# Two attention layers and two GLU layers on one core: four value parts folded instead of three, and the second output projection in two strips

## The chip, the core and the metric

The kernel runs on one core of a Trainium2 chip. The metric is the device time of one execution in microseconds, median over runs; lower is better. The core has TensorE (PE), VectorE (DVE), ScalarE (ACT), GpSimd (POOL) and SyncE (SP), which here only issues transfers. 16 DMA engines bring data from HBM into SBUF.

## The reference

Everything is float32. Two tokens (B = 2, one position each) pass through attention, a GLU block, the same attention again and the same GLU block again, each with a layer norm before it and a residual around it:

```python
def _A_ref(x, k_cache, v_cache, wq, wo):
    B, Sq, D = x.shape                      # 2, 1, 576
    H, Dh = 32, 128                         # caches: (2, 32, 8192, 128)
    q = (lambda x, *d: x.transpose(*d))((x @ wq).reshape(B, Sq, H, Dh), 0, 2, 1, 3)
    scores = jnp.einsum("bhqd,bhkd->bhqk", q, k_cache) * (Dh ** -0.5)
    p = _softmax(scores, axis=-1)
    o = jnp.einsum("bhqk,bhkd->bhqd", p, v_cache)
    return (lambda x, *d: x.transpose(*d))(o, 0, 2, 1, 3).reshape(B, Sq, H * Dh) @ wo

x = x + _A_ref(_layernorm(x, axis=-1), A_k_cache, A_v_cache, A_wq, A_wo)
x = x + _B_ref(_layernorm(x, axis=-1), B_w_gate, B_w_up, B_w_down)
x = x + _A_ref(_layernorm(x, axis=-1), A_k_cache, A_v_cache, A_wq, A_wo)
x = x + _B_ref(_layernorm(x, axis=-1), B_w_gate, B_w_up, B_w_down)
```

`_B_ref` is gelu(x @ w_gate) * (x @ w_up) @ w_down with an inner width of 4608. Each attention layer reads K and V of all 64 pairs of batch and head, 512 MB.

## The kernel before

**Items.** An attention layer goes through items in a fixed order, the second layer in the reverse order of the first. An item is two heads of one batch (30 items that `PAIRS` counts, the kernel's numbers 0 to 29) or one head (4 items, the end of layer 0 and the start of layer 1). K and V of a two-head item are 8 MB each; they lie in SBUF as 128 partitions of 128 rows of 128 numbers, cut into eight parts of 16 rows (`JC`; a part is 2048 numbers a partition).

**Scores.** `multiply` (L769) lets VectorE multiply K by the query, which is held in PSUM, in place, in three steps of three, three and two parts (6144, 6144 and 4096 numbers a partition). GpSimd then adds the upper half of each row to the lower (L798), and VectorE sums what is left to one score a row (`add_up`, L801). `peak` (L825), `highest` (L833) and `softmax` (L850 to L858) turn scores into weights in the tile `prz`, with small matmuls (L827, L835, L871) in between.

**Values.** PE multiplies the weights by V (`values`, L943), four matmuls of 512 columns a part, each into its own strip of 32 partitions of the accumulator `acc`. The last `FOLD` parts of V are not multiplied by PE in the items that `folds` names (numbers 3 to 26 in layer 0, 2 to 26 in layer 1, 49 in all). For those, `weigh` lets VectorE multiply V by the weights, which ScalarE has copied to PSUM as `share` (L905, multiplication at L911), and GpSimd adds the rows together in halves (L914) down to four rows; `folded` then adds these four rows with one matmul (L921). With `FOLD = 3` the first call of `weigh` takes one part, and the second two, and L916 joins the two.

**Order.** The engines run their instructions in the order in which the program writes them. In item n the loop writes: the last `add_up` and `peak` of the item before (p), the second `weigh` of the item before that (f), the first `multiply`, the next item's query (L687), `folded(f)`, the softmax of p, the second `multiply`, for every other item `gather` (L966, L967), for the others `inverse` (L877), `values` of p, the first `add_up`, the third `multiply`, the first `weigh` of p, the second `add_up`.

**Transfers.** SyncE issues all large transfers on one queue, in the order that `plan_first`, `plan_second` and `plan_mlp` write down, each as soon as its space is free. Space for the two-head items is three pairs of slots, each pair for one K or V. K of the next item (L168) goes where V of two items ago lay, so it waits for `folded`; V of this item goes where its own K lay, so it waits for its last `add_up`. An issue that waits holds up all issues behind it.

**Projection.** After the items, `project` multiplies the attention output (4 columns) by wo. In layer 1, wo comes in two pieces (`WIDE` is 16: 16 rows of 128, 576 columns), and each of the 16 rows is multiplied in four strips of 144 columns, one to each 32 partitions of `xps` (L1021). `add_to_x` (L589) adds the result to `x` in the same layout. Then the GLU of layer 1 begins: `norm`, and the gate and up products (L1203), whose weights are transferred in space that K, V and wo have left.

Of the kernel before, what the change touches and what calls it, by code (L numbers as in the profile page):

```python
# [15 lines left out]
P = 128  # L16
B = 2
# [3 lines left out]
D = 576  # L21
# [3 lines left out]
JC = 16  # L25
HALF = P // 2
# [9 lines left out]
CW = D // 4  # L36
# [7 lines left out]
END = RING + NPLACE * PLACE  # L44
HELD = 5
SPLIT = (18, 18, 12, 16)
FOLD = 3


class Item:  # L50
# [75 lines left out]
def decode_layers(ctx, tc, x_in, kc, vc, wq, wo, wg, wu, wd, out):  # L126
    nc = tc.nc
# [10 lines left out]
    x = consts.tile([P, CW], F32, name="x")  # L138
    nc.vector.memset(x, 0.0)
    for c in range(4):  # L140
        for s in range(2):
            lo = 32 * c + s * B
# [12 lines left out]
    def done(key):  # L155
        arena.free(key)
        pump()

    def part_at(at, n):
        return space[:, at:at + n]  # L160
# [177 lines left out]
    def groups(layer):  # L338
        return range(H // WIDE[layer])[::1 - 2 * layer]

    def name(kind, layer, n):

        return kind, 1 if n in (KEYS_HELD if kind == "k" else VALUES_HELD) else layer, n
# [119 lines left out]
    for b in range(B):  # L463
        rows = ident.rearrange("p (c v i r) -> p i r v c", c=4, v=4, i=2)[:, :, :, b, :]
# [38 lines left out]
    acc = psum1.tile([P, 2, 512], F32, name="acc")  # L503
# [5 lines left out]
    xps = bank[:, 0:CW]  # L509
# [6 lines left out]
    low = bank2[:, 4 * GH + P + 6:]  # L516
    share = low[:, :FOLD * JC]
    kept = psum1.tile([P, JC, DH], F32, name="kept")
# [69 lines left out]
    def add_to_x():  # L588
        nc.vector.tensor_add(x, xps, x)  # L589
# [22 lines left out]
    def attention(layer):  # L612
# [28 lines left out]
        if layer == 0:  # L641
            for us in GU[0]:
                w = ready.pop(("wq", 0, us[0])).rearrange("p (u w) -> p u w", w=4 * EQ)
# [193 lines left out]
        def weights_of(n):  # L837

            if ITEMS[n].heads == 2:
                return prz.rearrange("p a e -> p (a e)")  # L840
            return prz[:, n - PAIRS, :]
# [55 lines left out]
        def weigh(n, first):  # L897

            lo = ITEMS[n].parts - FOLD
            if first:  # L900
                of_halves = weights_of(n)[:, 8 + 4 * JC * lo:8 + 4 * JC * (lo + FOLD)]
                of_halves = of_halves.rearrange("p (g a e) -> p a g e", a=4, e=4)
                for i in range(2):
                    at = slice(i * HALF, i * HALF + HALF)
                    nc.scalar.copy(share[at].rearrange("p (g e) -> p g e", e=4), of_halves[at, i])  # L905
            begin, rows = (0, JC) if first else (JC, (FOLD - 1) * JC)
            at = arena.live[name("v", layer, n), lo][0]
            t = part_at(at, FOLD * PART).rearrange("p (j d) -> p j d", d=DH)
            of_rows = share[:, begin:begin + rows].unsqueeze(2).to_broadcast([P, rows, DH])
            u = t[:, begin:begin + rows]  # L910
            nc.vector.tensor_tensor(out=u, in0=u, in1=of_rows, op=ALU.mult)  # L911
            while rows > 4:
                rows //= 2
                nc.gpsimd.tensor_tensor(out=u[:, :rows], in0=u[:, :rows], in1=u[:, rows:2 * rows], op=ALU.add)  # L914
            if not first:
                nc.gpsimd.tensor_tensor(out=t[:, :4], in0=t[:, :4], in1=u[:, :4], op=ALU.add)  # L916

        def folded(n):

            key, lo = name("v", layer, n), ITEMS[n].parts - FOLD  # L920
            nc.tensor.matmul(  # L921
# [92 lines left out]
        def project(g):  # L1014

            w = ready.pop(("wo", layer, g)).rearrange("p (i c) -> p i c", c=D)
            n = WIDE[layer]
            o = oT.rearrange("p g i s b -> p (g i) (s b)")
            for i in range(n):
                for c in range(4):  # L1020
                    nc.tensor.matmul(  # L1021
                        xps[32 * c:32 * c + 2 * B, :], o[:, g * n + i, :], w[:, i, c * CW:(c + 1) * CW],
                        start=(g == groups(layer)[0] and i == 0), stop=(g == groups(layer)[-1] and i == n - 1),
                    )
            done(("wo", layer, g))
# [25 lines left out]
        for i, n in enumerate(seq):  # L1051
# [8 lines left out]
            first = layer == 1 and i == 1  # L1060
# [8 lines left out]
            if f is not None:  # L1069
                weigh(f, False)  # L1070
# [3 lines left out]
            for j, (k, m) in enumerate(us):  # L1074
# [28 lines left out]
                if j == 2 and i and folds(p):  # L1103
                    weigh(p, True)
# [12 lines left out]
        n, p = seq[-1], seq[-2]  # L1117
        add_up(n, *units(n)[-1])
        first, second = groups(layer)[:2]
# [5 lines left out]
        if layer == 0:  # L1125
            nc.scalar.copy(two, qs)
            project(first)
# [4 lines left out]
        if layer == 0:  # L1132
            project(second)

            third, fourth, fifth = groups(layer)[2:5]
            values(N - 1, 0, 2)
            for g in (third, fourth):
                project(g)
            for k in range(2, ITEMS[n].parts, 2):
                values(N - 1, k, k + 2)  # L1140
                if k + 2 == ITEMS[n].parts:
                    nc.scalar.copy(back, spare)
            gather(n)
            project(fifth)
            context(n)
            divide(n)
        else:
            values(N - 1)
            finish(n)
            regroup()  # L1150
        spread()
        for g in groups(layer)[5:] if layer == 0 else groups(layer):
            project(g)
        add_to_x()


    def write(engine):
# [3 lines left out]
    def mlp(layer):  # L1161
# [106 lines left out]
        if layer == 0:  # L1268
            idle_products(1, 0)

    attention(0)
    mlp(0)
    attention(1)
    mlp(1)
    write(nc.scalar)
# [27 lines left out]
```

## Time and profile before

| | |
|---|---|
| median of 3 runs | 2680.91 us (2680.71 to 2681.0) |
| profiled execution | 2680.4 us, span 2678.6 us |
| VectorE busy | 2086.9 us (78%) |
| GpSimd busy | 1797.4 us (67%) |
| PE busy | 848.9 us (32%) |
| read from HBM | 1152.39 MB |

The span is what the profiler saw from the first to the last instruction of the profiled execution. Busy shares are means over the whole span, in which attention fills all but the first part, a stretch in the middle and the last 100 us or so. The rows that the prediction quotes from the timeline give the start in us, the duration (of all instructions of a merged row), engine, line and operation, the tiles written and read with their shapes, and in brackets the idle time before it with what ended that.

### The profile page before, as it was taken

The numbers are of one execution on the slowest core, as the hardware profiler recorded it, in microseconds if no ns is written. First come the engines' busy times: TensorE is split into PE (matmuls) and PEld (weight loads), VectorE is DVE, ScalarE is ACT, GpSimd is POOL, SyncE is SP. The second block draws the span as 40 slices with busy tenths as digits, with TensorE's granted clock in tenths as the row PEclk, the third lists the DMA queues.
The fourth block names the chain that finished last, engine by engine and source line by source line (L and its number), as shares of the span: only waits on it lengthen the run. The fifth ranks groups of instructions, "written<-read, shape, count | busy, mean of one in ns | idle before, by whom it ended". The sixth has DMA issues, their size and how long they took to land.

```text
span 2678.6 us, 14389 instructions
## 1 busy us (share of the span) xinstructions
PE 848.9 (32%) x5550; PEld 269.3 (10%) x5550; DVE 2086.9 (78%) x916; ACT 185.0 (7%) x890; POOL 1797.4 (67%) x559
## 2 busy tenths in 40 slices
PE   1313232232223232334663322223222322222256
PEld 0100000000000000011221100000000000000022
DVE  4878888898888888867038779888888988888840
ACT  0000000000000000001026000000000000000000
POOL 2547787778778777844028458778887877787720
PEclk8666655665665566566986665566566556655678
DMA  9999999999999999999999999999999999999998
GB/s 423 437 429 434 435 433 433 433 436 433 431 435 434 430 436 431 434 429 426 419 417 432 435 437 429 434 434 433 433 433 436 430 433 437 428 436 436 430 431 383
DMA packets 29340, 1153.33 MB, mean 431 GB/s; under 512 B 3384, under 2 KB 3416, under 8 KB 4184
## 3 DMA queue, kind: packets, MB, share of 16 engines
q1 hardware_dynamic: 29088, 1152.40, 99.8%
q8 instruction: 43, 0.70, 0.1%
q14 instruction: 25, 0.20, 0.0%
q10 hardware_dynamic: 184, 0.02, 0.0%
HBM read 1152.39 MB, written 0.01 MB: 430 GB/s over the span
## 4 chain that ended last, share of the span: by engine, by line
DMA 70%; DVE 20%; PE 6%; POOL 3%; issue 1%; ACT 1%; SPq 0%; another core or an unknown queue 0%; POOLq 0%; ACTq 0%; DVEq 0%
DMA space<-in_A_k_cache_dram 61%; DVE space L769 17%; PE acc L921 3%; DMA space<-in_B_w_down_dram 2%; DMA space<-in_B_w_gate_dram 2%; DVE scores L801 2%; POOL space L798 2%; PE bank L687 2%; DMA space<-in_A_v_cache_dram 1%; DMA space<-in_B_w_up_dram 1%; PE bank L1262 1%; DMA space<-in_A_wo_dram 1%; ACT space L791 0%; DMA x<-in_A_x_dram 0%; POOL space L785 0%
## 5 line engine op out<-in xcount | busy, mean ns | idle before, releaser
L798 POOL TENSOR_TENSOR space<-space 128x3072 f32<-128x3072 f32 (+4 forms) x221 | 1128.7, 5108 | 371.2 <-DVE space L769 323.9
L769 DVE TENSOR_TENSOR space<-space,bank 128x6144 f32<-128x6144 f32 (+4 forms) x223 | 1111.9, 4987 | 320.9 <-DMA space<-in_A_k_cache_dram 245.8
L914 POOL TENSOR_TENSOR space<-space 128x1024 f32<-128x1024 f32 (+2 forms) x245 | 575.3, 2348 | 241.2 <-DVE space L911 229.7
L943 PE MATMUL acc<-space,prz 128*16 128x512 f32 (+1 forms) x2920 | 472.7, 812 | 430.2 <-DMA space<-in_A_v_cache_dram 422.1
L801 DVE TENSOR_REDUCE scores<-space 128x48 f32<-128x3072 f32 (+4 forms) x223 | 564.1, 2548 | 23.1 <-POOL space L798 22.9
L911 DVE TENSOR_TENSOR space<-space,bank 128x2048 f32<-128x2048 f32 x98 | 328.3, 3350 | 24.7 <-PE bank L827 24.7
L943 PEld LDWEIGHTS acc<-space,prz 128*16 128x16 f32 (+1 forms) x2920 | 98.1, 120 | 746.5 <-issue 496.8
L687 PE MATMUL bank<-qsb,home 36*128 36x128 f32 x60 | 23.4, 491 | 415.8 <-DVE space L769 397.8
L687 PE MATMUL bank<-qsb,wide 36*128 36x128 f32 x60 | 23.1, 486 | 400.3 <-DVE space L769 383.1
L850 ACT ACTIVATE nbs<-bank 128x2 f32<-128x2 f32 (+1 forms) x68 | 11.6, 171 | 1917.2 <-PE bank L835 1867.5
L585 POOL TENSOR_TENSOR rstd<-ve,few 128x1 f32<-128x1 f32 x4 | 2.2, 561 | 169.0 <-DVE ve L583 169.0
L827 PE MATMUL bank<-ident,m 128*1 128x128 f32 x68 | 21.8, 320 | 273.2 <-DVE m L825 273.1
L921 PE MATMUL acc<-space,few 128*16 128x512 f32 x98 | 92.5, 1047 | 14.2 <-POOL space L916 14.2
L1214 DVE STREAM_TRANSPOSE gu<-acc 128x288 f32<-128x288 f32 x4 | 1.9, 483 | 94.4 <-ACT acc L1212 94.4
L916 POOL TENSOR_TENSOR space<-space 128x512 f32<-128x512 f32 x49 | 62.1, 1267 | 3.8
L687 PEld LDWEIGHTS bank<-qsb,home 36*128 36x128 f32 x60 | 14.7, 304 | 424.8 <-DVE space L769 405.7
L687 PEld LDWEIGHTS bank<-qsb,wide 36*128 36x128 f32 x60 | 14.5, 300 | 408.8 <-DVE space L769 390.3
L858 ACT ACTIVATE prz<-scores,nbs 64x128 f32<-64x128 f32 (+1 forms) x128 | 50.7, 396 | 12.3 <-POOL prz L848 8.9
L791 ACT ACTIVATE space<-space 128x128 f32<-128x128 f32 x164 | 48.4, 296 | 19.7 <-DVE space L769 16.6
L589 DVE TENSOR_TENSOR x<-bank,x 128x144 f32<-128x144 f32 x4 | 1.2, 308 | 57.8 <-PE bank L1262 40.2
L980 PE MATMUL bank<-few,home 128*64 128x4 f32 (+2 forms) x136 | 17.1, 249 | 86.9 <-DVE home L967 86.9
L966 DVE TENSOR_TENSOR acc<-acc,few 128x512 f32<-128x512 f32 x34 | 23.5, 691 | 26.5 <-PE acc L943 26.5
(117 smaller groups left out, 602.8 us busy)
## 6 DMA issues: line engine op xcount, KB each, us to landing
space<-in_A_v_cache_dram SPq DMA_DIRECT2D x7, 4096.0 KB
space<-in_A_k_cache_dram SPq DMA_DIRECT2D x6, 4096.0 KB
space<-in_B_w_gate_dram SPq DMA_DIRECT2D x9, 1152.0 KB
space<-in_B_w_up_dram SPq DMA_DIRECT2D x9, 1152.0 KB
space<-in_B_w_down_dram SPq DMA_DIRECT2D x8, 1152.0 KB
space<-in_A_wq_dram SPq DMA_DIRECT2D x9, 1024.0 KB
space<-in_A_wo_dram SPq DMA_DIRECT2D x2, 4608.0 KB
space<-in_A_k_cache_dram SPq DMA_DIRECT2D x4, 2048.0 KB
```

What stands on the lines that cost most here:

```text
L687: nc.tensor.matmul(qb[n], of_row, qsb[rows, m * DH:(m + 1) * DH], start=True, stop=True)
L769: nc.vector.tensor_tensor(out=u[:, :r, :], in0=t[:, :r, :], in1=qb[n].unsqueeze(1).to_broadcast([P, r, DH]), op=ALU.mult)
L791: nc.scalar.activation(u[:, j, :], u[:, j, :], AF.Copy, accum_out=S[n][:, base(n, k) + j:base(n, k) + j + 1])
L798: nc.gpsimd.tensor_tensor(out=half, in0=half, in1=u[:, :r, DH // 2:], op=ALU.add)
L801: nc.vector.tensor_reduce(out=S[n][:, base(n, k):base(n, k) + own_rows(n, k, m)], in_=prod.pop((n, k)), axis=AX.X, op=ALU.add)
L858: nc.scalar.activation(pr[at, lo:].rearrange("p (g e) -> p g e", e=4)[:, 0:it.rows // 2 * it.heads:2 * it.heads, :], s[at, :it.rows].rearr ...
L911: nc.vector.tensor_tensor(out=u, in0=u, in1=of_rows, op=ALU.mult)
L914: nc.gpsimd.tensor_tensor(out=u[:, :rows], in0=u[:, :rows], in1=u[:, rows:2 * rows], op=ALU.add)
L916: nc.gpsimd.tensor_tensor(out=t[:, :4], in0=t[:, :4], in1=u[:, :4], op=ALU.add)
L921: nc.tensor.matmul(accumulator(n)[0:16, :], owner[:, 8 * ITEMS[n].b:8 * ITEMS[n].b + 16], part_at(arena.live[key, lo][0], 4 * DH), start=F ...
L943: nc.tensor.matmul(accumulator(n)[32 * c:32 * c + m, :], pr[:, at:at + m], t[g // 4][:, g % 4 * 4:g % 4 * 4 + 4, :].rearrange("p j d -> p ...
L1262: nc.tensor.matmul(xps[32 * c:32 * c + (2 * B if split else 17), :], hidden(v, e, i), w[:, k, c * CW:(c + 1) * CW], start=(n == 0 and k == ...
```

## The change

`FOLD` becomes 4, and both calls of `weigh` take two parts. PE multiplies four parts of V in those 49 items, and VectorE and GpSimd weight and fold the other four. In layer 1 `project` multiplies wo in two strips of 288 columns, to partitions 0 and 64 of the first half of `acc`; four adds on VectorE then bring the four quarters into `x`.

```diff
-FOLD = 3
+FOLD = 4
...
-            begin, rows = (0, JC) if first else (JC, (FOLD - 1) * JC)
+            rows = FOLD // 2 * JC
+            begin = 0 if first else rows
...
+            strips = (4, 2)[layer]
+            width = D // strips
             for i in range(n):
-                for c in range(4):
+                for c in range(strips):
+                    lo = P // strips * c
+                    to = acc[lo:lo + 2 * B, 0, :width] if layer else xps[lo:lo + 2 * B, :]
                     nc.tensor.matmul(
-                        xps[32 * c:32 * c + 2 * B, :], o[:, g * n + i, :], w[:, i, c * CW:(c + 1) * CW],
+                        to, o[:, g * n + i, :], w[:, i, c * width:(c + 1) * width],
                         start=(g == groups(layer)[0] and i == 0), stop=(g == groups(layer)[-1] and i == n - 1),
                     )
...
-        add_to_x()
+        if layer == 0:
+            add_to_x()
+        else:
+            for c in range(4):
+                to, of_half = x[32 * c:32 * c + 2 * B, :], acc[c // 2 * HALF:c // 2 * HALF + 2 * B, 0]
+                nc.vector.tensor_add(to, of_half[:, c % 2 * CW:(c % 2 + 1) * CW], to)
```

How the instructions stand in one item of the steady part of layer 0, on VectorE, before the change (`space` is the one large SBUF tile that holds K, V and weights, `bank` and `bank_125` are PSUM tiles, the first with the queries, the second with `share`):

```order
L769 TENSOR_TENSOR space<-space,bank 128x6144
L833 TENSOR_REDUCE m_427<-bank_125 1x2
L769 TENSOR_TENSOR space<-space,bank 128x6144
L966 TENSOR_TENSOR acc<-acc,few 128x512
L967 TENSOR_REDUCE home<-acc 128x128
L801 TENSOR_REDUCE scores<-space 128x48
L769 TENSOR_TENSOR space<-space,bank 128x4096
L911 TENSOR_TENSOR space<-space,bank_125 128x2048
L801 TENSOR_REDUCE scores<-space 128x48
L801 TENSOR_REDUCE scores<-space 128x32
L825 TENSOR_REDUCE m<-scores 128x1
L911 TENSOR_TENSOR space<-space,bank_125 128x4096
```

And the same item of the changed kernel, where the lines behind `weigh`'s edit have moved by one:

```order
L769 TENSOR_TENSOR space<-space,bank 128x6144
L833 TENSOR_REDUCE m_424<-bank_125 1x2
L769 TENSOR_TENSOR space<-space,bank 128x6144
L967 TENSOR_TENSOR acc<-acc,few 128x512
L968 TENSOR_REDUCE home<-acc 128x128
L801 TENSOR_REDUCE scores<-space 128x48
L769 TENSOR_TENSOR space<-space,bank 128x4096
L912 TENSOR_TENSOR space<-space,bank_125 128x4096
L801 TENSOR_REDUCE scores<-space 128x48
L801 TENSOR_REDUCE scores<-space 128x32
L825 TENSOR_REDUCE m<-scores 128x1
L912 TENSOR_TENSOR space<-space,bank_125 128x4096
```

The order is the same; the first weighting is twice as long. On GpSimd, from the first item that folds, before:

```order
L798 TENSOR_TENSOR space<-space 128x48x64 x2
L798 TENSOR_TENSOR space<-space 128x32x64
L914 TENSOR_TENSOR space<-space 128x1024
L914 TENSOR_TENSOR space<-space 128x512
L914 TENSOR_TENSOR space<-space 128x2048
L914 TENSOR_TENSOR space<-space 128x1024
L914 TENSOR_TENSOR space<-space 128x512
L916 TENSOR_TENSOR space<-space 128x512
L798 TENSOR_TENSOR space<-space 128x48x64 x2
```

And after:

```order
L798 TENSOR_TENSOR space<-space 128x48x64 x2
L798 TENSOR_TENSOR space<-space 128x32x64
L915 TENSOR_TENSOR space<-space 128x2048
L915 TENSOR_TENSOR space<-space 128x1024
L915 TENSOR_TENSOR space<-space 128x512
L915 TENSOR_TENSOR space<-space 128x2048
L915 TENSOR_TENSOR space<-space 128x1024
L915 TENSOR_TENSOR space<-space 128x512
L917 TENSOR_TENSOR space<-space 128x512
L798 TENSOR_TENSOR space<-space 128x48x64 x2
```

The first fold has one add more, of 2048 numbers, ahead of the two that it had; the second fold, the joining add and the adds of the next item behind it stand as they did. On PE each of these items has 16 matmuls at `values` for 20, and the projection of layer 1 has 64 for 128.

## The prediction

> **What bounds the kernel now.** I read the page's shares and slices first, then the chain of waits in order of time, then the timeline of single items.
>
> ```profile
> span 2678.6 us, 14389 instructions
> PE 848.9 (32%) x5550; PEld 269.3 (10%) x5550; DVE 2086.9 (78%) x916; ACT 185.0 (7%) x890; POOL 1797.4 (67%) x559
> ...
> DMA  9999999999999999999999999999999999999998
> ...
> HBM read 1152.39 MB, written 0.01 MB: 430 GB/s over the span
> ```
>
> The transfers never pause: every slice of the DMA row has a 9 but the last. No engine is over 78%, so the span is the time in which 1152 MB arrive. Less engine work can therefore gain nothing in the middle; more can lose something, if it delays an issue until the DMA queue is empty. What counts is how regularly items follow each other and how much slack each has. The chain of waits gives the starts of the first multiplication of an item (columns: start, duration, what):
>
> ```profile
> 219.74 6.57 DVE space L769
> ...
> 1111.65 6.57 DVE space L769
> ...
> 1608.73 6.57 DVE space L769
> ...
> 2461.91 6.57 DVE space L769
> ...
> 2500.61 6.57 DVE space L769
> ```
>
> From 219.74 to 1111.65 are 23 items, from 1608.73 to 2500.61 another 23: 38.78 us an item in both layers (891.9 / 23); the last quiet one took 38.70. That is the DMA's pace for one K and one V of 8 MB. All folding of values lies in these two stretches. One whole item on the timeline, with the end of the item before it (columns: start, duration, engine, line, operation, idle before):
>
> ```profile
> 1954.99 8.29 POOL L914 TENSOR_TENSOR space<-space 128x2048 f32<-128x2048 f32 x3 [4.75 <-DVE space L911]
> 1957.47 6.55 DVE L769 TENSOR_TENSOR space<-space,bank 128x6144 f32<-128x6144 f32 x1 [2.56 <-DMA space<-in_A_k_cache_dram]
> 1963.36 1.27 POOL L916 TENSOR_TENSOR space<-space 128x512 f32<-128x512 f32 x1
> ...
> 1964.57 6.71 POOL L798 TENSOR_TENSOR space<-space 128x3072 f32<-128x3072 f32 x1
> 1964.80 1.89 PE L921 MATMUL acc<-space,few 128*16 128x512 f32 x2
> ...
> 1966.72 0.33 SPq L168 DMA_DIRECT2D space<-in_A_k_cache_dram  x1
> ...
> 1971.47 3.32 DVE L801 TENSOR_REDUCE scores<-space 128x48 f32<-128x3072 f32 x1
> ...
> 1976.86 6.29 PE L943 MATMUL acc<-space,prz 128*16 128x512 f32 x40 [7.71 <-DMA space<-in_A_v_cache_dram]
> 1979.04 2.28 DVE L911 TENSOR_TENSOR space<-space,bank 128x2048 f32<-128x2048 f32 x1
> ...
> 1986.81 0.33 SPq L168 DMA_DIRECT2D space<-in_A_v_cache_dram  x1
> ...
> 1987.55 4.42 DVE L911 TENSOR_TENSOR space<-space,bank 128x4096 f32<-128x4096 f32 x1 [0.46 <-PE bank L827]
> 1992.05 6.93 POOL L914 TENSOR_TENSOR space<-space 128x2048 f32<-128x2048 f32 x2 [4.64 <-DVE space L911]
> 1996.18 6.55 DVE L769 TENSOR_TENSOR space<-space,bank 128x6144 f32<-128x6144 f32 x1 [4.21 <-DMA space<-in_A_k_cache_dram]
> ```
>
> VectorE still waits 2.56 and 4.21 us for K at the two L769. But look at GpSimd at the top: the fold (L914, L916) runs straight into the first L798 with no idle time. There is a ring through two engines: fold, L798, L801, the second L911, next fold. It is hidden today because it is shorter than 38.7 us.
>
> **The change part by part.** *First weighting, one part to two.* The first L911 becomes 128x4096, which is the shape of the second: 4.42 for 2.28, so VectorE has 2.14 us more in each of the 49 folded items. The second L911 and its fold stay as they are.
>
> *First fold on GpSimd.* It had adds of 1024 and 512 elements, and gains one of 2048:
>
> ```profile
> L798 POOL TENSOR_TENSOR space<-space 128x3072 f32<-128x3072 f32 x114 | 763.3, 6695 | 215.4 <-DVE space L769 173.6 <-issue 27.7 <-DVE m L833 12.3
> ...
> L914 POOL TENSOR_TENSOR space<-space 128x2048 f32<-128x2048 f32 x49 | 220.5, 4499 | 229.7 <-DVE space L911 229.7
> ```
>
> That is 4.50 us, and GpSimd waited 4.64 us there before the second fold (row 1992.05), a wait that itself grows by the 2.14. This part is hidden; without the cover it would cost its 4.50.
>
> *Four value matmuls less.* PE took 6.29 us for 20 at L943 and takes about 5.0 for 16. It had waited 7.71 us for V, so nothing comes of it.
>
> *The ring.* From L801 at 1971.47 to the fold at 1992.05 are 20.58 us. The next item but one needs a little more:
>
> ```profile
> 2514.61 3.32 DVE L801 TENSOR_REDUCE scores<-space 128x48 f32<-128x3072 f32 x1
> ...
> 2535.29 8.27 POOL L914 TENSOR_TENSOR space<-space 128x2048 f32<-128x2048 f32 x3 [4.74 <-DVE space L911]
> ```
>
> 20.68 us; I take 20.63. From the fold's start to L798 are 9.58 (1954.99 to 1964.57), L798 takes 6.70 (its mean above), and L801 follows after about 0.03. Before: 20.63 + 9.58 + 6.70 + 0.03 = 36.94, so 1.84 under the DMA's 38.78. After: 36.94 + 2.14 = **39.08**, over it by 0.30. From then on each item comes 0.30 us later than the DMA would allow.
>
> *Who waits for that.* SyncE issues in order. K waits for L921, which waits for the fold; V waits for the last L801 of the item. In the item above V was issued at 1986.81 and the second L911 ended at 1991.97, 5.16 later. So if that L911 ends x us after K has landed, V is issued only 5.16 - x before the queue runs empty. K is safer: it was issued at 1966.72, some 10 us before V landed (PE starts on V at 1976.86).
>
> *When the queue runs empty.* How early must an issue come? No row shows it for 8 MB. An issue alone takes 0.33 (row 1986.81); the last small output held SyncE 1.7 us:
>
> ```profile
> SPq L1299 <- DMA out_dram<-x: 1.7, 1, 1.7
> ```
>
> Bounds 0.33 and about 2; I take 1.7, since that is a whole small transfer. So 5.16 - 1.7 = 3.4 us of lateness are free. The Trainium skill (DMA: Bandwidth & Descriptors, Anatomy of one DMA) puts the fixed cost of a DMA issued from GpSimd at some 2 us, most of it the receipt after the last byte; by that price 3.2 us would be free and the sum 0.6 larger. The row agrees nearly; no row parts what lies before the first byte from the receipt.
>
> *The sum.* In an item with a gather L801 starts 15.25 us after L769 (16.4 when the ring holds it), as these rows show:
>
> ```profile
> 2010.82 0.69 DVE L967 TENSOR_REDUCE home<-acc 128x128 f32<-128x512 f32 x1
> 2011.43 3.34 DVE L801 TENSOR_REDUCE scores<-space 128x48 f32<-128x3072 f32 x1
> ```
>
> The second L911 then ends 15.25 + 20.58 - 0.08 + 2.14 = 37.9 us after that L769, 0.8 early. Layer 0: 23 rounds of the ring bring it to -0.8 + 23 x 0.30 = 6.1 late; 3.4 are free, 2.7 us are lost in empty queues. Layer 1: 24 rounds, 6.4 late, 3.0 lost. Lost DMA time is never made up: **+5.7 us**. The profiled execution took 2680.4 (its span of 2678.6 and 1.8 around it) and would take 2686.1; the median of the three runs lies 0.5 higher at 2680.91, and so the forecast at **2686.6 us**. The bounds: the queue's 0.33 would leave 4.8 us free and take 2.8 off the sum, 2 us would add 0.6; 0.1 more or less in the ring moves the sum by 47 x 0.1 = 4.7.
>
> *The projection in layer 1.* The rows of the tail:
>
> ```profile
> 2539.32 2.29 DVE L769 TENSOR_TENSOR space<-space,bank 128x2048 f32<-128x2048 f32 x1 [4.11 <-DMA space<-in_A_k_cache_dram]
> ...
> 2578.05 8.64 PE L943 MATMUL acc<-space,prz 128*16 128x512 f32 x64 [2.14 <-DMA space<-in_A_v_cache_dram]
> ...
> 2591.94 5.55 PE L1021 MATMUL bank<-space,oT 128*4 128x144 f32 x128 [0.41 <-DVE oT L1034]
> ...
> 2596.56 6.12 SPq L257 DMA_DIRECT2D space<-in_B_w_up_dram  x2
> 2600.16 4.10 PE L1021 MATMUL bank<-space,oT 128*4 128x144 f32 x128 [2.67 <-DMA space<-in_A_wo_dram]
> 2604.33 0.31 DVE L589 TENSOR_TENSOR x<-bank,x 128x144 f32<-128x144 f32 x1 [12.19 <-PE bank L1021]
> ...
> 2614.04 7.63 PE L1203 MATMUL acc<-space,xt 128*8 128x288 f32 x80 [8.38 <-DMA space<-in_B_w_gate_dram]
> ...
> 2624.76 5.91 PE L1203 MATMUL acc<-space,xt 128*8 128x288 f32 x64 [3.09 <-DMA space<-in_B_w_gate_dram]
> 2641.09 8.78 PE L1203 MATMUL acc<-space,xt 128*8 128x288 f32 x96 [10.42 <-DMA space<-in_B_w_up_dram]
> ```
>
> 128 records are 64 matmuls of 144 columns: 4.10 / 16 = 0.26 us for a set of four strips. Two strips of 288 are not in the trace. If only the total of columns counts, they cost the same 5.55 + 4.10 = 9.65; if strips run side by side, a set lasts as long as one strip of it, now twice as wide, 19.3 in all. I take 19.3, since width is what L1203's sets of four pay for: 8.78 / 12 = 0.73 us at 288 columns. The Trainium skill (TensorEngine Tiling (Array Packing), Tiling Modes) has four independent tiles of 32 columns but only two of 64, so that half the array's concurrency goes; by that the projection takes 19.3, and no row of before shows two strips. The add of x becomes four of at most 0.31 us (+0.9). K(0)'s chain comes later by 3.4 and by the 4.11 of DMA wait that is gone (2539.32), less the 2.14 that PE waited for V(0) at 2578.05: 5.4. So x is 9.7 + 0.9 + 5.4 = 16 us late against the DMA. PE waits 8.38 + 3.09 + 10.42 = 21.9 us for gate and up weights, which hides it all with 6 us to spare. The up weights wait for space that the projection frees; they were issued at 2596.56, 28 us before the gate weights ahead of them were in (2624.76), so that 16 us later still leaves 12. Cost 0.
>
> **The rivals.** *The ring closes under the DMA's pace (not slower).* Its place is the L798 behind the fold. If a round gains less than (3.4 + 0.8) / 23 = 0.18 us, that is if the ring is under 38.96, the lateness never uses up the free 3.4, and the time stays at 2680.9 us. For it: 0.12 us in 39 is all that decides, and VectorE alone needs only 37.9. Against it: each term is a repeated row with a spread of 0.1. Chance 0.27.
>
> *The ring is longer than its terms.* GpSimd and VectorE are now busy together for nearly all of an item. If the fold and L798 took 0.2 us more between them, the ring would be 39.28 and the 47 rounds 9.4 us longer: 2696 us. For it: nothing in the trace has both so full. Against: L798 keeps to 6695 ns in the mean beside VectorE today. Chance 0.12.
>
> *The two strips don't run side by side.* 64 matmuls of 288 columns at 0.73 are 46.7 us, 37 over before; x would be 37 + 0.9 + 5.4 = 43 us late, 21 more than PE's waits hold: 2707 us. Against: L1021's sets of four at 0.26. Chance 0.03.
>
> *Faster.* Behind the last weights PE has some 5 us of work, and nothing there is taken out; 5.4 us less has no source. Chance 0.02.
>
> **How the numbers follow.** The forecast (ring of 39.0 to 39.2, queue lost for 2 to 10 us) has the remaining 0.56, with a range of its own of 2683 to 2691. A measurement of this kernel tells about 0.2%, 5.4 us, from no change; the line is 2686.3, just under the forecast, so I give 0.32 of the 0.56 to the far side. Slower: 0.32 + 0.12 + 0.03 = 0.47; same: 0.24 + 0.27 = 0.51; faster 0.02. The range for 8 in 10 takes in the first rival and the bounds of the ring, and leaves out the upper half of the second and the third: 2680.4 to 2694.
>
> **What the profile after would show.** Right: the first weighting at 4.42; fold and L798 back to back in every item, and L801 released by L798; starts of the first L769 growing from 38.7 to 39.1 apart, without a wait for K in the later items; small dips in the GB/s row late in each layer; the projection near 19 us, with PE's waits for gate and up weights shortened. Wrong: L769 ending waits for K in every item (my ring is too long by then), or more time than now behind the last weights (the strips).

## The result and the profile after

The kernel after takes 2696.07 us (median of 6 runs, 2694.94 to 2697.57), the kernel before beside it 2680.75 (2680.36 to 2681.0): a ratio of 1.0057 with a 95% interval of 1.0045 to 1.007. It is 15.3 us slower, where 5.7 were forecast; the range ended at 2694.0. The profiled execution took 2694.94 us, 1.8 more than its span. First the page of the kernel after:

```profile
span 2693.1 us, 13402 instructions
PE 808.9 (30%) x5030; PEld 254.3 (9%) x5030; DVE 2196.9 (82%) x919; ACT 186.3 (7%) x890; POOL 2016.1 (75%) x608
...
DMA  9999999999999999999999999999999999999999
...
HBM read 1152.39 MB, written 0.01 MB: 428 GB/s over the span
...
DVE 46%; POOL 30%; DMA 16%; issue 4%; PE 3%; ACT 1%; POOLq 0%; ACTq 0%; SPq 0%; DVEq 0%
...
L769 DVE TENSOR_TENSOR space<-space,bank 128x6144 f32<-128x6144 f32 (+4 forms) x223 | 1111.7, 4986 | 150.1 <-DMA space<-in_A_k_cache_dram 75.6
...
L801 DVE TENSOR_REDUCE scores<-space 128x48 f32<-128x3072 f32 (+4 forms) x223 | 565.2, 2553 | 97.1 <-POOL space L798 97.1
```

The DMA row is still all 9s, and 430 GB/s have become 428. What changed is the chain that ended last: DVE and POOL now hold 46% and 30% of it. The same line of the page of the kernel before, and the same two groups there:

```profile
DMA 70%; DVE 20%; PE 6%; POOL 3%; issue 1%; ACT 1%; SPq 0%; another core or an unknown queue 0%; POOLq 0%; ACTq 0%; DVEq 0%
...
L769 DVE TENSOR_TENSOR space<-space,bank 128x6144 f32<-128x6144 f32 (+4 forms) x223 | 1111.9, 4987 | 320.9 <-DMA space<-in_A_k_cache_dram 245.8
...
L801 DVE TENSOR_REDUCE scores<-space 128x48 f32<-128x3072 f32 (+4 forms) x223 | 564.1, 2548 | 23.1 <-POOL space L798 22.9
```

VectorE's wait for K at L769 fell from 245.8 to 75.6 us, and its wait for GpSimd's L798 at L801 rose from 22.9 to 97.1. A ring through two engines sets the pace where the transfers did. One turn of it on the timeline after, between the first and the last V issue at that pace (columns: start, duration, engine, line, operation, idle before):

```profile
1649.40 0.33 SPq L168 DMA_DIRECT2D space<-in_A_v_cache_dram  x1
...
1945.31 3.35 DVE L801 TENSOR_REDUCE scores<-space 128x48 f32<-128x3072 f32 x1 [0.37 <-POOL space L798]
...
1962.80 0.33 SPq L168 DMA_DIRECT2D space<-in_A_v_cache_dram  x1
...
1963.65 4.42 DVE L912 TENSOR_TENSOR space<-space,bank 128x4096 f32<-128x4096 f32 x1 [0.56 <-PE bank L827]
1967.99 6.55 DVE L769 TENSOR_TENSOR space<-space,bank 128x6144 f32<-128x6144 f32 x1
1968.15 8.31 POOL L915 TENSOR_TENSOR space<-space 128x2048 f32<-128x2048 f32 x3 [2.31 <-DVE space L912]
...
1976.54 1.27 POOL L917 TENSOR_TENSOR space<-space 128x512 f32<-128x512 f32 x1
1977.77 13.34 POOL L798 TENSOR_TENSOR space<-space 128x3072 f32<-128x3072 f32 x2
...
1984.48 3.35 DVE L801 TENSOR_REDUCE scores<-space 128x48 f32<-128x3072 f32 x1 [2.06 <-POOL space L798]
...
2550.42 0.33 SPq L168 DMA_DIRECT2D space<-in_A_v_cache_dram  x1
```

L769 at 1967.99 waits for nothing: K is there before VectorE. From L801 to the fold are 22.84 us, from there to L798 9.62, and the next L801 follows 6.71 later: 39.17. From 1649.40 to 2550.42 are 23 turns of 39.174 us. Before, an item took 38.78. Behind the last of these turns in layer 0, L769 waits for K in both kernels, and starts at 1150.37 us before and at 1158.29 after: of the 14.5 us by which the span grew, 7.9 were lost in layer 0.

### The profile page after: what moved, and what is told of

Its sections match the earlier page's. It is cut to its first block, busy times and chain, and to the rows that moved or that the text cites. A ratio compares the mean times of both kernels' runs of the same rounds, so it can differ in the third digit from the quotient of the medians.

```text
span 2693.1 us, 13402 instructions
## 1 busy us (share of the span) xinstructions
PE 808.9 (30%) x5030; PEld 254.3 (9%) x5030; DVE 2196.9 (82%) x919; ACT 186.3 (7%) x890; POOL 2016.1 (75%) x608
## 4 chain that ended last, share of the span: by engine, by line
DVE 46%; POOL 30%; DMA 16%; issue 4%; PE 3%; ACT 1%; POOLq 0%; ACTq 0%; SPq 0%; DVEq 0%
DVE scores L801 17%; DVE space L912 15%; POOL space L915 14%; POOL space L798 13%; DVE space L769 12%; DMA space<-in_A_k_cache_dram 11%; DMA space<-in_B_w_down_dram 2%; POOL space L917 2%; DMA space<-in_B_w_up_dram 1%; DMA space<-in_A_wo_dram 1%; PE bank L827 1%; PE acc L1026 1%; DVE m L825 1%; DMA x<-x 0%; ACT space L791 0%
## 5 line engine op out<-in xcount | busy, mean ns | idle before, releaser
L798 POOL TENSOR_TENSOR space<-space 128x3072 f32<-128x3072 f32 (+4 forms) x221 | 1126.1, 5105 | 286.2 <-DVE space L769 248.9
L769 DVE TENSOR_TENSOR space<-space,bank 128x6144 f32<-128x6144 f32 (+4 forms) x223 | 1111.7, 4986 | 150.1 <-DMA space<-in_A_k_cache_dram 75.6
L915 POOL TENSOR_TENSOR space<-space 128x2048 f32<-128x2048 f32 (+2 forms) x294 | 797.8, 2713 | 128.0 <-DVE space L912 112.7
L801 DVE TENSOR_REDUCE scores<-space 128x48 f32<-128x3072 f32 (+4 forms) x223 | 565.2, 2553 | 97.1 <-POOL space L798 97.1
L944 PE MATMUL acc<-space,prz 128*16 128x512 f32 (+1 forms) x2528 | 424.5, 836 | 330.6 <-DMA space<-in_A_v_cache_dram 322.5
L912 DVE TENSOR_TENSOR space<-space,bank 128x4096 f32<-128x4096 f32 x98 | 433.0, 4418 | 27.2 <-PE bank L827 27.2
L944 PEld LDWEIGHTS acc<-space,prz 128*16 128x16 f32 (+1 forms) x2528 | 86.1, 122 | 610.0 <-issue 428.1
L687 PE MATMUL bank<-qsb,home 36*128 36x128 f32 x60 | 23.4, 491 | 333.2 <-DVE space L769 320.1
L687 PE MATMUL bank<-qsb,wide 36*128 36x128 f32 x60 | 23.1, 486 | 317.6 <-DVE space L769 304.0
L917 POOL TENSOR_TENSOR space<-space 128x512 f32<-128x512 f32 x49 | 62.1, 1268 | 3.8
L827 PEld LDWEIGHTS bank<-ident,m 128*1 128x1 f32 x68 | 5.4, 79 | 576.6 <-issue 520.4
L791 ACT ACTIVATE space<-space 128x128 f32<-128x128 f32 x164 | 48.4, 296 | 19.7 <-DVE space L769 14.8
L687 PEld LDWEIGHTS bank<-qsb,home 36*128 36x128 f32 x60 | 14.7, 303 | 343.6 <-DVE space L769 329.3
L687 PEld LDWEIGHTS bank<-qsb,wide 36*128 36x128 f32 x60 | 14.5, 299 | 327.3 <-DVE space L769 312.5
L835 PE MATMUL bank<-m,few 1*128 1x2 f32 (+1 forms) x136 | 39.0, 354 | 15.1 <-DVE m L833 15.1
```

The costliest lines, as they stand in the source:

```text
L687: nc.tensor.matmul(qb[n], of_row, qsb[rows, m * DH:(m + 1) * DH], start=True, stop=True)
L769: nc.vector.tensor_tensor(out=u[:, :r, :], in0=t[:, :r, :], in1=qb[n].unsqueeze(1).to_broadcast([P, r, DH]), op=ALU.mult)
L791: nc.scalar.activation(u[:, j, :], u[:, j, :], AF.Copy, accum_out=S[n][:, base(n, k) + j:base(n, k) + j + 1])
L798: nc.gpsimd.tensor_tensor(out=half, in0=half, in1=u[:, :r, DH // 2:], op=ALU.add)
L801: nc.vector.tensor_reduce(out=S[n][:, base(n, k):base(n, k) + own_rows(n, k, m)], in_=prod.pop((n, k)), axis=AX.X, op=ALU.add)
L827: nc.tensor.transpose(mT[n], m, ident)
```

## The experiments

Each is compared with runs of the kernel before on the same chip (medians 2680.68 to 2680.77).

**One part alone.** The fold of four parts with wo in four strips as before:

```diff
-            strips = (4, 2)[layer]
-            width = D // strips
...
-                for c in range(strips):
+                for c in range(4):
```

> The changed kernel with the projection of layer 1 as before (four strips of 144): only the fold's half of the change. Theory A (the ring fold, L798, L801, second weighting is 39.17 us against the DMA's 38.7 to 38.8, and empties the queue): the whole loss stays, 2694 to 2697 us. Theory B (the wider strips reach the end): the loss goes or shrinks clearly, 2681 to 2688 us. Theory C (both): between, 2688 to 2694.

2697.88 us, ratio 1.0064 (1.0047 to 1.0081), 0.9 over the upper end of what was written for theory A and 1.8 over the kernel after. And the two strips with the fold of three parts (`FOLD = 3` and its `begin, rows` as before):

> The kernel before with the projection of layer 1 in two strips of 288: only the other half of the change. Theory A: 2680.4 to 2681.4 us, the 8 us that the projection is longer are hidden behind waits for gate and up weights. Theory B: 2686 to 2696 us.

2680.70 us, ratio 1.0 (0.999 to 1.0009). The whole loss is the fold's. What the strips did is seen in the tail of the kernel after:

```profile
2611.27 17.68 PE L1026 MATMUL acc<-space,oT 128*4 128x288 f32 x128 [0.41 <-DVE oT L1039]
...
2629.00 1.24 DVE L1164 TENSOR_TENSOR x<-acc,x 4x144 f32<-4x144 f32 x4 [17.52 <-PE acc L1026]
...
2632.95 6.72 PE L1213 MATMUL acc<-space,xt 128*8 128x288 f32 x80 [1.69 <-issue]
...
2640.61 4.35 PE L1213 MATMUL acc<-space,xt 128*8 128x288 f32 x64 [0.94 <-DMA space<-in_B_w_gate_dram]
...
2656.85 7.77 PE L1213 MATMUL acc<-space,xt 128*8 128x288 f32 x96 [11.89 <-DMA space<-in_B_w_up_dram]
```

The projection takes 17.68 us instead of 9.65. The first L1213 no longer waits for weights (8.38 before), and the second waits 0.94 instead of 3.09; but the third still waits 11.89, so nothing of it comes through.

**One add less on the ring, and one less off it.** The last halving is left out of the second fold (e3, on the ring) or of the first (e4, off it), 1.27 us each; rows 4 to 7 of that fold are then missing from the output:

```diff
-            while rows > 4:
+            while rows > (4 if first else 8):
```

> The changed kernel without the last halving (8 rows to 4, an add of 512 numbers, 1.27 us on GpSimd) of the second fold, which lies on the ring; the rows 4 to 7 of it are left out of the result. Theory A: the ring is 39.17 - 1.27 = 37.9 us and under the DMA's pace again, so the whole loss goes: 2680.5 to 2682 us. Theory D (VectorE and GpSimd are too full, or disturb each other, wherever the work lies): 49 adds less give back a few per cent of GpSimd's extra work, 2691 to 2695 us.

> The changed kernel without the last halving (8 rows to 4, an add of 512 numbers, 1.27 us on GpSimd) of the first fold, which is not on the ring; the rows 4 to 7 of it are left out of the result. The same work is removed as from the second fold in the kernel beside it. Theory A: nothing changes, 2694 to 2697 us. Theory D: the same as there, 2691 to 2695 us, with the two kernels equal.

Leaving it out off the ring gives nothing: 2696.44 us, ratio 1.0059 (1.0044 to 1.0074). On the ring the same add, left out, gives back 9 of the 15 us: 2687.18 (2686.75 to 2688.3), ratio 1.0024 (1.0015 to 1.0034). So place counts, not how full GpSimd is. But 6.5 us stayed, which my theory did not expect. The timeline of the kernel with the shorter ring shows what happened in the item where the queries change:

```profile
607.14 6.55 DVE L769 TENSOR_TENSOR space<-space,bank 128x6144 f32<-128x6144 f32 x1 [1.57 <-DMA space<-in_A_k_cache_dram]
...
613.61 0.43 DVE L668 COPY wide<-few 128x128 f32<-128x128 f32 x1
613.92 6.65 POOL L798 TENSOR_TENSOR space<-space 128x3072 f32<-128x3072 f32 x1
613.96 6.69 DVE L668 COPY home<-few 128x128 f32<-128x128 f32 x1
...
651.23 6.55 DVE L769 TENSOR_TENSOR space<-space,bank 128x6144 f32<-128x6144 f32 x1
```

A copy of 128x128 elements took 6.69 us, as long as the L798 beside it, and the next item began 44.1 us later instead of 38.7. In the kernel before, the second copy had begun 0.08 us ahead of L798, and was not held up:

```profile
613.82 0.22 DVE L668 COPY home<-few 128x128 f32<-128x128 f32 x1
613.90 6.70 POOL L798 TENSOR_TENSOR space<-space 128x3072 f32<-128x3072 f32 x1 [1.07 <-issue]
```

The same happens once in layer 1. The Trainium skill (SBUF — State Buffer, SBUF: two separate sides) has VectorE and GpSimd share a pair of ports under an exclusive lock, where the loser stands still for the whole instruction; the 6.69 us beside 6.65 agree. The next run moves only these copies, `pairs_of` at L668, to ScalarE, with the shorter ring kept:

```diff
-                nc.vector.tensor_copy(
+                nc.scalar.copy(
```

> The kernel after with the last halving of the second fold left out, as in the run with the shorter ring (so rows 4 to 7 of that fold are missing from its output), and the small copies of L668 (128x128, from SBUF to SBUF, some 0.2 us each) made by ScalarE instead of VectorE. Theory of the copy: the shorter ring still lost 6.5 us because, once per layer, such a copy on VectorE stood still for as long as GpSimd's L798 ran beside it (6.69 us beside 6.65), which made one trip of the ring about 46 us long and emptied the queue; moved to ScalarE it no longer stands in the ring, and the time falls from 2687.2 to 2680.5 to 2682. Rival, the shortened ring itself is still too long or the queue runs dry for another reason: the time stays at 2685 to 2688.

2682.26 us (2681.38 to 2682.94), ratio 1.0005 (0.9996 to 1.0015): 4.9 of the 6.5 us went with the copies. The median is 0.26 over the upper end of what I had written, and 1.5 over the time before. The chain of waits shows where that comes from: in layer 0 the last L769 of the stretch that folds starts at 1111.61 (1111.65 before), and in layer 1 the first and the last at 1610.74 and 2502.48 (1608.73 and 2500.61 before). So the turns of the ring lose nothing any more, and some 2 us are lost ahead of layer 1's stretch. To see whether these copies had a part in the loss of the kernel after itself, the same edit was made there alone:

> The kernel after with the small copies of L668 on ScalarE and nothing else changed; it parts the two edits of the run with two matmuls and no join. In the kernel after these copies took 0.74 and 0.21 us, so they can have cost it little. Theory (the ring of 39.18 us is the whole loss of the kernel after): 2694 to 2697, no change from it. Rival (the copies cost the kernel after what they cost the run with the shorter ring, some 3 us a layer): 2689 to 2691.

2699.0 us (2697.67 to 2700.98), ratio 1.0066 (1.0049 to 1.0083). Taking them off VectorE gained nothing there; on ScalarE they cost rather more (2.9 us over the kernel after, against my expectation of no change). Most of it comes at the start of layer 1. In the kernel after, the copies on VectorE are over in time for the next L769:

```profile
1432.99 0.22 DVE L668 COPY home<-few 128x128 f32<-128x128 f32 x1
...
1434.04 1.74 DVE L769 TENSOR_TENSOR space<-space,bank 128x1536 f32<-128x1536 f32 x1
```

On ScalarE they stand behind seven activations of L791 that it works through first, and L769 waits for them, through the matmul of L687:

```profile
1436.75 0.29 ACT L668 COPY home<-few 128x128 f32<-128x128 f32 x1
1437.10 0.48 PE L687 MATMUL bank<-qsb,home 36*128 36x128 f32 x2 [4.28 <-ACT home L668]
...
1437.62 1.75 DVE L769 TENSOR_TENSOR space<-space,bank 128x1536 f32<-128x1536 f32 x1 [2.23 <-PE bank L687]
```

From the L769 ahead of the copies to this one are 4.90 us (from 1432.72) for 2.86 (from 1431.18) in the kernel after, so 2.0 of the 2.9 us arise here. The 2 us at the same place in the run before this one fit that.

**The whole sum with a shorter ring.** The add that joins the two folds (L917) is left out, and PE multiplies both folded rows instead; the copies are on ScalarE:

```diff
-            if not first:
-                nc.gpsimd.tensor_tensor(out=t[:, :4], in0=t[:, :4], in1=u[:, :4], op=ALU.add)
...
+            for k in (0, FOLD // 2):
+                nc.tensor.matmul(
...
+                    part_at(arena.live[key, lo + k][0], 4 * DH), start=False,
+                    stop=k > 0 and completes(seq.index(n)),
```

> The kernel after, without the GpSimd add that joins the two folds (L917): TensorE multiplies both folded rows instead, one matmul more per item; and the L668 copies on ScalarE. The ring is shorter by that add, 1.27 us, with the whole sum still formed. Theory of the ring and the copy together: the ring is 37.9 us, under the 38.75 that the transfers take, and the time is that of the kernel before, 2680.5 to 2682. Rival, something else in the fourth part's fold costs: 2685 to 2696.

2681.85 us (2680.8 to 2682.99), ratio 1.0004 (0.9994 to 1.0013), with the first weighting still of two parts; the copies on ScalarE cost it their 2 us at the start of layer 1 as well (L769 at 1112.00 and 1610.79). On its timeline:

```profile
1959.13 8.30 POOL L915 TENSOR_TENSOR space<-space 128x2048 f32<-128x2048 f32 x3 [2.23 <-DVE space L912]
1959.69 6.55 DVE L769 TENSOR_TENSOR space<-space,bank 128x6144 f32<-128x6144 f32 x1 [0.63 <-DMA space<-in_A_k_cache_dram]
...
1967.39 13.36 POOL L798 TENSOR_TENSOR space<-space 128x3072 f32<-128x3072 f32 x2
```

Fold to L798 is 8.26 us instead of 9.62, and L769 waits for K again (0.63): the ring is back under the transfers' pace.

**One add more on the ring.** An add of the join's size, on rows that nobody reads again, behind the join:

```diff
                 nc.gpsimd.tensor_tensor(out=t[:, :4], in0=t[:, :4], in1=u[:, :4], op=ALU.add)
+                nc.gpsimd.tensor_tensor(out=u[:, 4:8], in0=u[:, 4:8], in1=u[:, :4], op=ALU.add)
```

> The kernel after with one more GpSimd add of the size of the join (1.27 us, on rows that nobody reads again) behind it, on the ring; the result is not changed. Theory of the ring: 39.18 + 1.27 = 40.44 us a trip against 38.78 of the transfers, 1.67 lost per item; two layers of 23 and 24 rounds less 1.7 and the 0.8 at the start each lose some 73 us in all: 2750 to 2758. Rival, the loss of the kernel after is a fixed one for each layer (some stall at its start) and not a rate per item: below 2705.

2748.62 us (2747.75 to 2749.81), ratio 1.0254 (1.0238 to 1.0269), just under what was written and far from the rival's 2705. First and last V issue at its pace:

```profile
1675.57 0.33 SPq L168 DMA_DIRECT2D space<-in_A_v_cache_dram  x1
...
2604.51 0.33 SPq L168 DMA_DIRECT2D space<-in_A_v_cache_dram  x1
```

23 turns of 40.39 us. The loss is a rate per item, and it follows the ring.

**How much notice the queue needs.** In the kernel before, V's issue is held until the second weighting is done. The ring stays as it was (36.94 us); only the issue comes later:

```diff
+            if held:
+                key = held[0][0]
+                one_column = ready.pop(key)[held[0][1]][:, 0, 0:1]
+                nc.vector.tensor_tensor(out=one_column, in0=one_column, in1=share[:, 0:1], op=ALU.mult)
+                while held:
+                    done(held.pop(0))
```

> The kernel before, with the next item's V transfer held back until the weighting of the second part has ended, so that it is handed to the queue some 2.5 and 4.0 us (one item and the next) ahead of the last bytes of the transfer in front of it, instead of some 8 to 9; the ring of the kernel before keeps its length, and nothing else is moved. My forecast's step (a notice of 1.7 us is enough): 2680.5 to 2682, no change. Theory of the long notice (a transfer needs some 3.5 us from its issue until all 16 DMA engines have it): every other item loses 0.5 to 1 us, over some 48 items 10 to 30 us, 2692 to 2710.

2703.19 us (2702.24 to 2704.09), ratio 1.0084 (1.0069 to 1.0099): 22.4 us slower with every engine's work as before but 49 one-column products. V issues on the timeline:

```profile
2005.95 0.33 SPq L168 DMA_DIRECT2D space<-in_A_v_cache_dram  x1
...
2047.58 0.33 SPq L168 DMA_DIRECT2D space<-in_A_v_cache_dram  x1
...
2084.89 0.33 SPq L168 DMA_DIRECT2D space<-in_A_v_cache_dram  x1
...
2125.76 0.33 SPq L168 DMA_DIRECT2D space<-in_A_v_cache_dram  x1
...
2163.25 0.33 SPq L168 DMA_DIRECT2D space<-in_A_v_cache_dram  x1
...
2204.54 0.33 SPq L168 DMA_DIRECT2D space<-in_A_v_cache_dram  x1
```

And the first multiplication of each item in the chain of waits (start, duration, what), which here starts when the K ahead of that V has landed:

```profile
2011.58 6.57 DVE space L769
2050.26 6.57 DVE space L769
2089.77 6.56 DVE space L769
2128.60 6.57 DVE space L769
...
2168.23 6.56 DVE space L769
...
2206.94 6.57 DVE space L769
2247.55 6.56 DVE space L769
```

Set side by side, with the loss against the quiet 38.70:

| V issued ahead of L769 by | next item after | lost |
|---|---|---|
| 5.63 | 38.68 | 0 |
| 2.68 | 39.51 | 0.8 |
| 4.88 | 38.83 | 0.1 |
| 2.84 | 39.63 | 0.9 |
| 4.98 | 38.71 | 0 |
| 2.40 | 40.61 | 1.9 |

With some 5 us of notice nothing is lost; with 2.4 to 2.8 it costs 0.8 to 1.9 us. Lead and loss add up to 3.5 to 4.3 us in the lossy rows: that is, as an estimate, what this queue wants, where I had taken 1.7.

The packets of the kernel after show where most of that goes. In the traces each of these transfers ends with 16 packets of under 512 bytes, which I read as one from each of the 16 DMA engines. V was issued at 1962.80; the first row below is the stretch from 1964.30 to 1964.90, the second the one from 1964.30 to 1967.00:

```profile
DMA packets 14, 0.39 MB, mean 655 GB/s; under 512 B 8, under 2 KB 8, under 8 KB 8
...
DMA packets 33, 1.11 MB, mean 413 GB/s; under 512 B 16, under 2 KB 16, under 8 KB 16
```

Half of the engines are through with K 1.5 to 2.1 us behind V's issue, and the last only 4.1 us behind it. A lead that is counted to the landing of K, as the prediction and the table count it, is thus some 2.6 us longer than the lead that the first engine has. Some of the rest is the start itself: in the kernel with the longer ring no packet of data begins in the first 0.9 us behind V's issue (1958.30 to 1959.20).

## Why the prediction was right in kind and too small

**The bound and the ring: right.** The terms were the ones named: the first weighting at 4.42, fold and L798 back to back, L801 released by L798, L769 without a wait for K. The two runs with the ring 1.27 us shorter (once the copies were out of its way) end within 1.5 us of the time before, and that rest lies outside the ring, at the start of layer 1; the one with the ring 1.22 us longer loses 67.9.

**The ring's length: short by 0.09.** Forecast 39.08, measured 39.17. From L801 to the fold 22.84, where 20.63 + 2.14 = 22.77 stood: I had averaged two kinds of item (20.58 and 20.68), and ring-bound items are all like the slower kind. From the fold to L798 9.62 for 9.58. At 47 turns that is (39.174 - 39.08) x 47 = 4.4 us, as the prediction's own rate of 4.7 for 0.1 says.

**The free lateness: the step that failed.** The prediction put it so: "I take 1.7, since that is a whole small transfer. So 5.16 - 1.7 = 3.4 us of lateness are free." With the measured pace, 47 turns run (39.174 - 38.78) x 47 = 18.5 us over, less 0.8 at each layer's start leaves 16.9. Of these 15.3 were lost; so only 1.6, or 0.8 a layer, were free. Two layers at 3.4 - 0.8 are 5.2 us. Together: 5.7 + 4.4 + 5.2 = 15.3. That sum must come out, since the 0.8 is what the loss left over; what speaks for it is measured elsewhere: layer 0 alone lost 7.9 us where the prediction gave it 2.7, and the run with V's issue held back, whose ring is under the pace, lost 22.4. The kernel with the longer ring gives the same sum another end: (40.39 - 38.78) x 47 - 1.6 = 74.1 us over, 67.9 lost, so 3.1 a layer were free before it settled. The lateness is not a stock that is free until it is used up. By these sums, which are estimates, the queue loses 0.4 us an item at a lead of 5.16 - 0.8 = 4.4 us and 1.6 at 5.16 - 3.1 = 2.1; each kernel drifts to the lead at which it loses what its ring is over. The packets agree roughly with the estimates: over six turns around the one shown, the last of the 16 that end K comes 4.0 to 5.1 us behind V's issue in the kernel after, and 1.7 to 3.5 in the one with the longer ring. The row I used (1.7 for the last small output) spoke of another thing; the bounds of 0.33 and 2 that I put around it didn't hold the value. The Trainium skill's 2 us (DMA: Bandwidth & Descriptors, Anatomy of one DMA), given there for issues from GpSimd, was too short here as well: a lead of 2.4 to 2.8 still lost 0.8 to 1.9. What the step left out is that the queue does not run empty at one moment: the first engine is done with K some 2.6 us ahead of the last.

The loss shows where I said to look, in the page's GB/s row, though faintly and from early in each layer on, not only late. It has the rate in 40 equal slices of the span. The row before, and the row after:

```profile
GB/s 423 437 429 434 435 433 433 433 436 433 431 435 434 430 436 431 434 429 426 419 417 432 435 437 429 434 434 433 433 433 436 430 433 437 428 436 436 430 431 383
...
GB/s 421 436 435 434 432 430 433 421 433 424 434 424 431 425 431 427 433 427 428 421 413 437 433 431 434 432 427 432 430 426 425 433 423 433 425 430 426 433 430 391
```

In the slices from the eighth to the seventeenth the mean is 433 GB/s before and 428 after, about the ratio of 38.78 to 39.17.

**What was called hidden: right.** The first fold's longer chain gave nothing back when an add was left out of it, and the strips took 17.68 us for 19.3 forecast and cost nothing, as PE's waits for gate and up weights took it up. The value matmuls had no run of their own.

**The rivals.** The ring did not close under the DMA's pace: it was 39.17, against 38.96 as the point of decision. "The ring is longer than its terms" had the time that came out, 2696, but not the cause: GpSimd and VectorE did not slow each other by 0.2, and of the 9.6 us over the forecast the ring's length is 4.4. The strips ran side by side.

What stays open: the last 0.9 of the 2.9 us that the copies on ScalarE cost the kernel after, why the 16 engines do not end a transfer together, and how the loss grows between a lead of 5 us and one of 2.4. No version tried beats the kernel before; the one with two matmuls and no join equals it within its interval.

## What to carry to other kernels

In a kernel whose transfers never pause, look for the longest ring of waits through the engines and compare it with the pace of the transfers: it may grow for nothing up to that pace, and beyond it each item pays the difference. Measure the notice that the queue needs by holding one issue back in the kernel itself, since an issue that is "still in time" by a few us may already cost. A full DMA row does not show that the queue loses; the chain of waits does, and the GB/s row by 1%.

## What the hardware showed that I had not expected

An 8 MB transfer issued 2.4 to 2.8 us before VectorE could start on the one ahead of it lost 0.8 to 1.9 us; at some 5 us it lost nothing. The 16 packets that end the transfer looked at lay over 2.6 us, so a lead that is counted to the landing holds for the last engine only. And a copy of 128x128 elements from SBUF to SBUF on VectorE, 0.22 us by itself, took 6.69 us when a GpSimd instruction of 6.65 us had started just ahead of it; VectorE's L769, which also ran beside GpSimd, showed no such stall (4986 ns in the mean after, 4987 before).
